# A 64-point transform and two MLPs on one core: the prologue's copies, weight loads and conversions in another order

## The chip, the cores and the metric

The kernel runs on one core of one Trainium2 chip. A core has five engines with an instruction queue each: TensorE (PE in the rows; PEld is its weight load), VectorE (DVE), ScalarE (ACT), GpSimd (POOL) and SyncE (SP), which here only issues DMAs. The 16 DMA engines are shared by all queues. [...] The metric is device time in microseconds (us).

## The reference

What is computed: the real part of a two-dimensional Fourier transform of x (2 batches, 3008 positions, 256 channels), then two MLPs over its 6016 tokens.

```python
X = np.fft.fft(np.fft.fft(x, axis=1), axis=2).real          # (2, 3008, 256) -> tokens (6016, 256)
h = X @ moe_w_in                                            # 256 -> 2048
g = np.maximum(h, 0) + moe_alpha * np.minimum(h, 0)
y = g @ moe_w_out                                           # 2048 -> 256
h2 = y @ moe2_w_in
out = (h2 / (1 + np.exp(-h2))) @ moe2_w_out
```

The host hands the weights over as 64-bit words; the kernel loads them raw and converts them to float32 pairs itself.

## The kernel before

The 3008 positions are split as 47 x 64. A product over the 47 (the position products, tile `psU`) is followed by one over the 64 (tile `psB`), and the transform over channels is folded into the first MLP's input weights (tile `psW`: the product of a converted weight `wq` with the constants `cwt`, split into a high and a low part `wa`). Tokens come in six groups of up to 512 columns; each of the six runs 16 steps of the first MLP (lines 575 to 621), and after all of them the second MLP runs in a second loop (lines 741 to 809). Everything is written in program order (`manual_schedule`); each engine works through its queue in that order, and the framework adds the semaphore waits that the data demand.

The change touches only the prologue, which ends where the loop `for c in range(NC)` begins. In order:

- Ten products of a zero tile (`spin`, line 894) go to PE while the inputs travel.
- SP loads `ac` (the constants of the position products), then the eight parts of x for batch 0, 8 positions each, 384 KB each. Behind part 5 comes the first raw weight, called i0 here (512 KB, the first 256 columns of the first MLP's `w_in`); behind part 7 the raw weights o0 (of `w_out`) and i1 (of `w_in`); then small constants and nine more raw weights. DMAs on SP take eight semaphores in turn, so each issue waits until the DMA eight earlier has landed. ACT issues the loads of `cwt` and `cbt`.
- `stage_u(n)` takes the next n positions (a chunk; `UNITS` lists them: five of 12, one of 4): two PE instructions per position into one of two `psU` buffers (three PSUM banks each), then four copies into `u_all`, alternately by DVE and ACT. Each copy reads one half of psU's partitions (`half`) and writes one half of u_all's (`m`).
- A conversion is a generator (`narrow`, line 203). Its work: two ACT instructions (lines 224 and 225) on the raw words, then three of DVE (230, 232, 234), then `finish`. For `w_out` that is an ACT copy (line 278) and a GpSimd subtraction (line 279). `next` runs it to its next `yield`, `run` to its end. i0 is converted behind chunk 3; psW and its sums psS (line 537) follow behind chunk 4, then the last chunk, then o0's conversion.
- `psB` (line 968): 32 instructions; ACT and DVE split the result into `pq`. A product `psP` (line 979) makes `pb`, ACT copies it, then i1 is converted (`run(first[1])`), and the loop begins: `psh` products (line 575), then on DVE lines 583, 584, 586, 589, and so on. The second psW is the loop's first job.

The tiles `ac`, `con` and `y64` (the float32 result of a conversion) share the two buffers of the tag "y".

```python
for i, (half, m) in enumerate(((0, 0), (1, 0), (0, 1), (1, 1))):
    src = v[half * N2:(half + 1) * N2, :, :, m].rearrange("p b j c -> p c b j")
    dst = uv[m * N2:(m + 1) * N2, :, half, done:done + n].rearrange("p c (b j) -> p c b j", j=4)
    if i % 2: A.activation(dst, src, AF.Copy)
    else: V.tensor_copy(dst, src)
```

Of the kernel before, what the change touches and what calls it, by code (L numbers as in the profile page):

```python
# [30 lines left out]
NX = 8  # L31
# [65 lines left out]
def kernel(  # L97
# [14 lines left out]
    nc = tc.nc  # L112
# [752 lines left out]
    T2 = 14, 16, 19, 22, 50, 51, 52, 53, 54, 56, 58  # L865
    SUB = G
    STEP2 = [0] + [NC * NF + 56 * c for c in range(NC - 1)]
    SPIN = 10,

    BEHIND = 5  # L870
    UNITS = 12, 12, 12, 12, 12, 4
    RAWS = {"o0": (0, "wA2"), "o1": (1, "wA2"), "i2": (0, "px1"), "i3": (1, "px1"), "i4": (0, "wA3"), "i5": (1, "wA3"),
            "o2": (0, "px2"), "o3": (1, "px2"), "i6": (0, "px6"), "i7": (1, "px6")}
    RAW_ORDER = ("i", 2), ("o", 1), ("i", 3), ("o", 2), ("i", 4), ("o", 3), ("i", 5), ("i", 6), ("i", 7)
# [6 lines left out]
    with tc.manual_schedule():  # L881
# [21 lines left out]
        def load_raw(kind, n):  # L903
            i, tag = RAWS[kind + str(n)]
            if tag not in places:
                places[tag] = keep.tile([P, 2, 2, 256, 2], I32, name="raw8", tag=tag)
            raws[kind, n] = t = places[tag][:, i]
            load64(rows_win(n) if kind == "i" else rows_wout(w_out, n), t)

        first = [narrow_win(p) for p in range(2)]  # L910
        for i in range(nx):
            if i % 2 == 0:
                t = keep.tile([2 * NP1, 2, NX, P], F32, name="x0", tag=f"wo1_{i // 2}")
            xr.append(t[:, i % 2])
            nc.sync.dma_start(xr[i], x[0, i])
            if i == BEHIND:
                next(first[0])
        A.dma_start(cwt.rearrange("p k e j -> p (k e j)"), cw)
        A.dma_start(cbts.rearrange("p a e k -> p (a e k)"), cb)
        load_raw("o", 0)  # L920
        next(first[1])
        con = wtile([2 * NP1, 192], F32, "const", "y")
        nc.sync.dma_start(con, ca)
        nc.sync.dma_start(al, alpha)
# [6 lines left out]
        def stage_u(n):  # L931

            nonlocal done
            t = pp.tile([P, 3, 512], F32, name="psU", tag="u", bufs=2)
            for j in range(n):
                i, r = divmod(done + j, NX)
                T.matmul(t[:, j // 4, j % 4 * 96:j % 4 * 96 + 96], xr[i][:, r], ac, start=True, stop=True)  # L937
            v = t[:, :n // 4, :384].rearrange("p b (j m c) -> p b j m c", j=4, m=2)
            for i, (half, m) in enumerate(((0, 0), (1, 0), (0, 1), (1, 1))):
                src = v[half * N2:(half + 1) * N2, :, :, m].rearrange("p b j c -> p c b j")  # L940
                dst = uv[m * N2:(m + 1) * N2, :, half, done:done + n].rearrange("p c (b j) -> p c b j", j=4)
                if i % 2:
                    A.activation(dst, src, AF.Copy)
                else:
                    V.tensor_copy(dst, src)
            done += n

        for i, n in enumerate(UNITS):
            stage_u(n)
            if i == 3:  # L950
                run(first[0])
            if i == 4:
                run(mix_w(0, pp, "o"))
        assert done == N2
        wo0 = narrow_wout(w_out, wo1, "wo1_", 0, 0, raws["o", 0])
        pre.__exit__(None, None, None)
        psh = ctx.enter_context(tc.tile_pool(name="psh", bufs=1, space=PSUM, reuse_waits="tile"))
        pso = ctx.enter_context(tc.tile_pool(name="pso", bufs=4, space=PSUM, reuse_waits="tile"))
        run(wo0)
        ur, cbt = u_all[:, 0], side(0)  # L960
        V.tensor_copy(cat.rearrange("p s m -> p (s m)"), con)
        row = wtile([P, CK, N2], F32, "row0", "h")
# [2 lines left out]
        for eo in range(2):  # L965
# [9 lines left out]
                A.activation(hi, src, AF.Copy)  # L975
            for src, hi, lo in pairs:
                V.tensor_tensor(lo, src, f32(hi), op=ALU.subtract)
        ps = pso.tile([P, CK, N2], F32, name="psP", tag="o")
        T.matmul(ps, ones[:, 0:1].to_broadcast([P, P]), row, start=True, stop=True)
        for dst, src in spread(0, lambda k0, k1, w: ps[:, k0:k1, :w]):  # L980
            A.activation(dst.rearrange("p (k c) -> p k c", c=src.shape[2]), src, AF.Copy)
        A.activation(rest, ps[:, 0, OWN:K20], AF.Copy)
        run(first[1])
        V.tensor_scalar(al, al, -1.0, 1.0, op0=ALU.mult, op1=ALU.add)


# [132 lines left out]
```

## Time and profile before

| what | before |
|---|---|
| median of three timed runs | 993.22 us (992.76 to 995.02) |
| the profiled execution, device time | 992.17 us |
| its span (first to last instruction) | 990.4 us |
| PE busy | 960.8 us, 97% of the span |
| DVE, ACT, POOL busy | 711.6, 592.9, 509.6 us |
| first position product | 5.74 us |
| first psB product | 29.39 us |
| first line 583 on DVE | 41.58 us |

Times in rows are microseconds from the span's start. A row of the timeline gives start, duration, engine, line, operation, output and inputs, shapes and count; in brackets stand the engine's idle time before it and what ended it. [...]

### The profile page before, as it was taken

To read this page: it belongs to the slowest core of one execution; us is meant where nothing else is said; L and a number is where in the kernel's file an instruction comes from. 1 tells how busy PE (TensorE), PEld (TensorE's weight loads), DVE (VectorE), ACT (ScalarE), POOL (GpSimd) and SP (SyncE) were. 2 spreads that over 40 slices of the span, in tenths; PEclk is the share of its full clock that TensorE was granted. 3 is DMA by queue.
4 is the path that set the end of the run, shared out by engine and by line. 5 is a ranking of instruction groups with operands and counts; after the bars stand their busy time and mean duration, and the time that the engine had idled before them with its cause. 6 is when DMAs were issued, how large, how long until landed. Compare 5 with 4: busy or idle time off the path is not lost.

```text
span 990.4 us, 12453 instructions
## 1 busy us (share of the span) xinstructions
PE 960.8 (97%) x4374; PEld 798.8 (81%) x4374; DVE 711.6 (72%) x1099; ACT 592.9 (60%) x1002; POOL 509.6 (51%) x328
## 2 busy tenths in 40 slices
PE   8889899999999999999999999999999999999998
PEld 7778778878878878778789988888888888888886
DVE  3598876779989988998766765576576567657554
ACT  3566556666656656665676565665566465565554
POOL 0144557765545546988996543354354354335222
PEclk9799999999999999999999999999999999999999
DMA  9400113333334210010011020010001001001001
GB/s 284 161 1 22 40 33 81 80 81 93 107 117 118 75 64 23 22 64 22 11 44 32 1 80 1 0 43 1 1 1 43 1 1 43 1 1 44 1 0 43
DMA packets 30430, 46.52 MB, mean 47 GB/s; under 512 B 3264, under 2 KB 13344, under 8 KB 30112
## 3 DMA queue, kind: packets, MB, share of 16 engines
q1 hardware_dynamic: 30080, 45.34, 14.9%
q8 instruction: 34, 0.56, 0.2%
q10 hardware_dynamic: 288, 0.39, 0.1%
q14 instruction: 28, 0.23, 0.1%
HBM read 32.22 MB, written 13.51 MB: 46 GB/s over the span
## 4 chain that ended last, share of the span: by engine, by line
PE 80%; DVE 8%; ACT 4%; POOL 3%; issue 2%; DMA 1%; SPq 0%; ACTq 0%; DVEq 0%; POOLq 0%
PE pso L809 26%; PE psh L741 23%; PE pso L621 18%; PE psh L575 9%; DVE r L589 3%; POOL gl L606 2%; ACT r L585 2%; DVE psh L584 1%; PE psB L413 1%; PE psW L531 1%; ACT gh L605 1%; PE psB L968 1%; PE psU L937 1%; DVE h L583 1%; DVE x L633 1%
## 5 line engine op out<-in xcount | busy, mean ns | idle before, releaser
L762 DVE TENSOR_TENSOR ring<-ring,psh 128x512 f32<-128x512 f32 (+1 forms) x336 | 222.3, 674 | 170.5 <-PE psh L741 161.2
L809 PE MATMUL pso<-ghl,wAo 128*128 128x512 f32 (+1 forms) x1152 | 310.7, 386 | 0.0
L606 POOL TENSOR_TENSOR gl<-r,gh 128x1024 fp32r<-128x1024 f32 (+1 forms) x96 | 227.1, 2366 | 153.6 <-ACT gh L605 117.2
L741 PE MATMUL psh<-ts,wi 128*128 128x512 f32 (+1 forms) x1008 | 280.8, 387 | 0.0
L753 POOL TENSOR_TENSOR ghl<-ring,ghl 128x512 fp32r<-128x512 f32 (+1 forms) x96 | 137.8, 1436 | 254.8 <-ACT ghl L748 181.6
L809 PEld LDWEIGHTS pso<-ghl,wAo 128*128 128x128 f32 x1152 | 216.3, 188 | 42.2
L765 ACT ACTIVATE ring<-ring 128x512 f32<-128x512 f32 (+1 forms) x192 | 119.4, 622 | 178.3 <-DVE ring L762 176.0
L741 PEld LDWEIGHTS psh<-ts,wi 128*128 128x128 f32 x1008 | 189.2, 188 | 36.7 <-DVE r L589 0.2
L621 PE MATMUL pso<-gh,wo_o 128*128 128x512 f32 (+1 forms) x768 | 189.4, 387 | 3.6 <-POOL wo_o L279 3.6
L575 PE MATMUL psh<-pq,wa 128*128 128x512 f32 (+1 forms) x576 | 167.9, 401 | 4.7 <-DVE r L589 4.6
L621 PEld LDWEIGHTS pso<-gh,wo_o 128*128 128x128 f32 x768 | 144.0, 188 | 33.1 <-POOL wo_o L279 4.7
L589 DVE SCALAR_TENSOR_TENSOR r<-r,al,psh 128x512 f32<-128x512 f32 (+1 forms) x192 | 134.0, 734 | 15.9 <-ACT r L585 4.8
L605 ACT ACTIVATE gh<-r 128x1024 fp32r<-128x1024 f32 (+1 forms) x96 | 100.3, 1044 | 68.0 <-DVE r L589 67.7
L575 PEld LDWEIGHTS psh<-pq,wa 128*128 128x128 f32 x576 | 106.1, 190 | 29.1 <-DVE r L589 8.4
L748 ACT ACTIVATE ghl<-ring 128x512 fp32r<-128x512 f32 (+1 forms) x192 | 119.0, 620 | 6.2
L585 ACT ACTIVATE r<-psh 128x512 f32<-128x512 f32 (+1 forms) x96 | 56.4, 588 | 82.8 <-DVE psh L584 77.0
L621 PE MATMUL pso<-gl,wo_o 128*128 128x512 f32 (+1 forms) x384 | 103.5, 391 | 1.9 <-POOL gl L606 1.9
L584 DVE TENSOR_TENSOR psh<-h,psh 128x512 f32<-128x512 f32 (+1 forms) x96 | 65.8, 685 | 47.4 <-PE psh L575 43.1
L621 PEld LDWEIGHTS pso<-gl,wo_o 128*128 128x128 f32 x384 | 72.0, 188 | 18.3 <-POOL gl L606 3.6
L753 DVE TENSOR_TENSOR ghl<-ring,ghl 128x512 fp32r<-128x512 f32 (+1 forms) x96 | 76.9, 802 | 4.0 <-ACT ghl L748 3.6
L583 DVE SCALAR_TENSOR_TENSOR h<-pb,wst,psh 128x512 f32<-128x512 f32 (+1 forms) x96 | 70.0, 730 | 0.0
L586 DVE TENSOR_TENSOR psh<-h,psh 128x512 f32<-128x512 f32 (+1 forms) x96 | 65.1, 679 | 0.0
(91 smaller groups left out, 668.0 us busy)
## 6 DMA issues: line engine op xcount, KB each, us to landing
raw<-in_w_in SPq DMA_DIRECT2D x16, 512.0 KB, 6.3
raw<-in_w_out SPq DMA_DIRECT2D x16, 512.0 KB, 3.8
out_dram<-ob SPq DMA_DIRECT2D x20, 256.0 KB, 2.2
x<-in_x SPq DMA_DIRECT2D x8, 384.0 KB, 9.6
xr<-in_x SPq DMA_DIRECT2D x16, 192.0 KB, 2.5
tmid<-ev SPq DMA_DIRECT2D x48, 64.0 KB, 1.8
ur<-tmid SPq DMA_DIRECT2D x12, 256.0 KB, 3.7
stash_o<-y SPq DMA_DIRECT2D x8, 256.0 KB, 4.0
```

The source lines that it names most:

```text
L575: T.matmul(t[:, :w], wa[q][:, mm, eo, a, :], pq[c][:, 2 * eo + bb, :w], start=n == 0, stop=n == 2)
L583: V.scalar_tensor_tensor(t[:, :w], pb[c][:, :w], wst[:, m, 0:1], ps[0][:, :w], op0=ALU.mult, op1=ALU.add)
L589: V.scalar_tensor_tensor(r[:, s, :w], r[:, s, :w], al[:, m:m + 1], ps[s][:, :w], op0=ALU.mult, op1=ALU.add)
L605: A.activation(hi[:, :, :w], r[:, :, :w], AF.Copy)
L606: G.tensor_tensor(lo[:, :, :w], r[:, :, :w], f32(hi[:, :, :w]), op=ALU.subtract)
L621: T.matmul(po[c][s][k][:, :w], wo1[q][:, mm, a, k * P:(k + 1) * P], g[:, s, :w], start=m == 0 and a == 0 and g is hi, stop=m == NF - 1 and ...
L741: T.matmul(bank[j][:, :w], wi2[p][:, FORMS[j], a], t[:, :w], start=a == 0 and t is hi, stop=t is lo)
L748: A.activation(outs[p, i][:, 0, :w], g[:, :w], AF.Copy)
L753: eng.tensor_tensor(hl[:, 1, :w], g[:, :w], f32(hl[:, 0, :w]), op=ALU.subtract)
L762: V.tensor_tensor(dst[:, :w], a[:, :w], bank[j][:, :w], op=ALU.add)
L765: A.activation(a[:, :w], a[:, :w], AF.Silu)
L809: T.matmul(po[c, 2][s][k][:, :w], wo2[q][:, mm + m, a, k * P:(k + 1) * P], outs[p, i][:, g, :w], start=p == 0 and i < 2 and a == 0 and g == 0,
```

## The change

`SPIN` goes from 10 to 5. Part 0 of x is loaded in two DMAs of 4 positions. The raw weights i0, o0 and i1 are issued behind parts 2, 3 and 4 of x. `UNITS` becomes four chunks of 12, one of 8 and two of 4. The four copies of a chunk are paired in another order, so that DVE writes the lower half of u_all's partitions and ACT the upper half. `AMONG` lists how many steps of which conversion (0: i0, 1: i1, 2: o0) are run behind which chunk, and psW for i0 comes behind chunk 3 instead of chunk 4. The rest of o0's conversion is run between the two halves of psB, and i1's no longer stands ahead of the loop.

```diff
@@ -865,10 +865,11 @@
     T2 = 14, 16, 19, 22, 50, 51, 52, 53, 54, 56, 58
     SUB = G
     STEP2 = [0] + [NC * NF + 56 * c for c in range(NC - 1)]
-    SPIN = 10,
-
-    BEHIND = 5
-    UNITS = 12, 12, 12, 12, 12, 4
+    SPIN = 5,
+
+    BEHIND = {2: ("i", 0), 3: ("o", 0), 4: ("i", 1)}
+    UNITS = 12, 12, 12, 12, 8, 4, 4
+    AMONG = {0: ((0, 3),), 1: ((0, 3),), 2: ((1, 1),), 3: ((1, 5),), 4: ((2, 1),), 6: ((2, 4),)}
     RAWS = {"o0": (0, "wA2"), "o1": (1, "wA2"), "i2": (0, "px1"), "i3": (1, "px1"), "i4": (0, "wA3"), "i5": (1, "wA3"),
             "o2": (0, "px2"), "o3": (1, "px2"), "i6": (0, "px6"), "i7": (1, "px6")}
     RAW_ORDER = ("i", 2), ("o", 1), ("i", 3), ("o", 2), ("i", 4), ("o", 3), ("i", 5), ("i", 6), ("i", 7)
@@ -912,13 +913,16 @@
             if i % 2 == 0:
                 t = keep.tile([2 * NP1, 2, NX, P], F32, name="x0", tag=f"wo1_{i // 2}")
             xr.append(t[:, i % 2])
-            nc.sync.dma_start(xr[i], x[0, i])
-            if i == BEHIND:
-                next(first[0])
+            for a, n in ((0, NX),) if i else ((0, NX // 2), (NX // 2, NX // 2)):
+                nc.sync.dma_start(xr[i][:, a:a + n], x[0, i, :, a:a + n])
+            if i in BEHIND:
+                kind, n = BEHIND[i]
+                if kind == "i":
+                    next(first[n])
+                else:
+                    load_raw(kind, n)
         A.dma_start(cwt.rearrange("p k e j -> p (k e j)"), cw)
         A.dma_start(cbts.rearrange("p a e k -> p (a e k)"), cb)
-        load_raw("o", 0)
-        next(first[1])
         con = wtile([2 * NP1, 192], F32, "const", "y")
         nc.sync.dma_start(con, ca)
         nc.sync.dma_start(al, alpha)
@@ -936,7 +940,7 @@
                 i, r = divmod(done + j, NX)
                 T.matmul(t[:, j // 4, j % 4 * 96:j % 4 * 96 + 96], xr[i][:, r], ac, start=True, stop=True)
             v = t[:, :n // 4, :384].rearrange("p b (j m c) -> p b j m c", j=4, m=2)
-            for i, (half, m) in enumerate(((0, 0), (1, 0), (0, 1), (1, 1))):
+            for i, (half, m) in enumerate(((0, 0), (0, 1), (1, 0), (1, 1))):
                 src = v[half * N2:(half + 1) * N2, :, :, m].rearrange("p b j c -> p c b j")
                 dst = uv[m * N2:(m + 1) * N2, :, half, done:done + n].rearrange("p c (b j) -> p c b j", j=4)
                 if i % 2:
@@ -945,18 +949,18 @@
                     V.tensor_copy(dst, src)
             done += n
 
+        wo0 = narrow_wout(w_out, wo1, "wo1_", 0, 0, raws["o", 0])
         for i, n in enumerate(UNITS):
             stage_u(n)
+            for g, k in AMONG.get(i, ()):
+                for _ in range(k):
+                    next(first[g] if g < 2 else wo0, 0)
             if i == 3:
-                run(first[0])
-            if i == 4:
                 run(mix_w(0, pp, "o"))
         assert done == N2
-        wo0 = narrow_wout(w_out, wo1, "wo1_", 0, 0, raws["o", 0])
         pre.__exit__(None, None, None)
         psh = ctx.enter_context(tc.tile_pool(name="psh", bufs=1, space=PSUM, reuse_waits="tile"))
         pso = ctx.enter_context(tc.tile_pool(name="pso", bufs=4, space=PSUM, reuse_waits="tile"))
-        run(wo0)
         ur, cbt = u_all[:, 0], side(0)
         V.tensor_copy(cat.rearrange("p s m -> p (s m)"), con)
         row = wtile([P, CK, N2], F32, "row0", "h")
@@ -975,12 +979,13 @@
                 A.activation(hi, src, AF.Copy)
             for src, hi, lo in pairs:
                 V.tensor_tensor(lo, src, f32(hi), op=ALU.subtract)
+            if eo == 0:
+                run(wo0)
         ps = pso.tile([P, CK, N2], F32, name="psP", tag="o")
         T.matmul(ps, ones[:, 0:1].to_broadcast([P, P]), row, start=True, stop=True)
         for dst, src in spread(0, lambda k0, k1, w: ps[:, k0:k1, :w]):
             A.activation(dst.rearrange("p (k c) -> p k c", c=src.shape[2]), src, AF.Copy)
         A.activation(rest, ps[:, 0, OWN:K20], AF.Copy)
-        run(first[1])
         V.tensor_scalar(al, al, -1.0, 1.0, op0=ALU.mult, op1=ALU.add)
 
 
```

What this does to the queues. First DVE, from the first position product on: the copies of chunks 0 to 2 before (`psU_148`, `psU_165`, `psU_182`), with the semaphores that each waits for.

```order
L945 COPY u_all_80<-psU_148 64x48x12 [waits PE_49]
L945 COPY u_all_80<-psU_148 64x48x12 [waits Activation_49]
L945 COPY u_all_80<-psU_165 64x48x12 [waits PE_49]
L945 COPY u_all_80<-psU_165 64x48x12 [waits Activation_49]
L945 COPY u_all_80<-psU_182 64x48x12 [waits PE_49]
```

The same place after the change (`psU_144`, `psU_165`, `psU_184` are chunks 0 to 2; `wq_161` is i0's result).

```order
L949 COPY u_all_80<-psU_144 64x48x12 [waits PE_49]
L949 COPY u_all_80<-psU_144 64x48x12 [waits Activation_49]
L230 TENSOR_SCALAR wq_161<-wq_161 128x512 [waits Activation_49]
L949 COPY u_all_80<-psU_165 64x48x12 [waits PE_49]
L949 COPY u_all_80<-psU_165 64x48x12 [waits Activation_49]
L232 ISA wq_161<-raw64_113,wq_161 128x1024 [waits DMAHW7_49,DVE_49]
L234 SCALAR_TENSOR_TENSOR wq_161<-raw64_113,wq_161 128x512 [waits DVE_49]
L949 COPY u_all_80<-psU_184 64x48x12 [waits PE_49]
```

The conversion of i0 now stands between the copies; a chunk's second DVE copy waits for ACT in both.

Next ACT around the last chunks, before: `psU_222` is chunk 4, `psU_251` chunk 5, the last; `y64_267` is o0's result.

```order
L943 ACTIVATE u_all_80<-psU_222 64x48x12 [waits DVE_49] x2
L533 ACTIVATE wa0_239<-psW_240 128x2x2x128 [waits PE_49]
L538 ACTIVATE wst_74<-psS_246 128x4 [waits PE_49]
L943 ACTIVATE u_all_80<-psU_251 64x48x4 [waits DVE_49] x2
L224 ACTIVATE y64_267<-raw8_128 128x512 [waits DMAHW4_49]
L225 ACTIVATE raw8_128<-raw8_128 128x512
L278 ACTIVATE wo1_o0_273<-y64_267 128x2x256 [waits DMAHW2_49,DVE_49]
```

After: `psU_204` is chunk 3, `psU_236` chunk 4, `psU_252` and `psU_261` chunks 5 and 6; `wq_201` is i1's result, `y64_249` o0's.

```order
L224 ACTIVATE wq_201<-raw64_120 128x512 [waits DMAHW3_49]
L225 ACTIVATE raw64_120<-raw64_120 128x512
L947 ACTIVATE u_all_80<-psU_204 64x48x12 [waits DVE_49] x2
L533 ACTIVATE wa0_224<-psW_225 128x2x2x128 [waits PE_49]
L538 ACTIVATE wst_74<-psS_231 128x4 [waits PE_49]
L947 ACTIVATE u_all_80<-psU_236 64x48x8 [waits DVE_49] x2
L224 ACTIVATE y64_249<-raw8_116 128x512 [waits DMAHW1_49,PE_49]
L225 ACTIVATE raw8_116<-raw8_116 128x512
L947 ACTIVATE u_all_80<-psU_252 64x48x4 [waits DVE_49] x2
L947 ACTIVATE u_all_80<-psU_261 64x48x4 [waits DVE_49] x2
```

Line 224 for o0 moved from behind the last chunk's copies to ahead of the copies of the last two, and it now waits for PE too: the last product of chunk 6, which reads the buffer that `y64_249` takes over.

Last SP, from the first part of x on, before (`x0` are the parts, two to a tile; `raw64_121` is i0, `raw8_128` o0, `raw64_130` i1).

```order
L915 DMA x0_112<-in_x 96x1024 x2
L915 DMA x0_115<-in_x 96x1024 x2
L915 DMA x0_118<-in_x 96x1024
L915 DMA x0_118<-in_x 96x1024 [waits DMAHW0_49]
L196 DMA raw64_121<-in_w_in 128x2x512 [waits DMAHW1_49]
L915 DMA x0_123<-in_x 96x1024 [waits DMAHW2_49]
L915 DMA x0_123<-in_x 96x1024 [waits DMAHW3_49]
L196 DMA raw8_128<-in_w_out 128x2x512 [waits DMAHW4_49]
L196 DMA raw64_130<-in_w_in 128x2x512 [waits DMAHW5_49]
```

After (`raw64_113` is i0, `raw8_116` o0, `raw64_120` i1).

```order
L917 DMA x0_107<-in_x 96x512 x2
L917 DMA x0_107<-in_x 96x1024
L917 DMA x0_111<-in_x 96x1024
L196 DMA raw64_113<-in_w_in 128x2x512
L917 DMA x0_111<-in_x 96x1024 [waits DMAHW0_49]
L196 DMA raw8_116<-in_w_out 128x2x512 [waits DMAHW1_49]
L917 DMA x0_118<-in_x 96x1024 [waits DMAHW2_49]
L196 DMA raw64_120<-in_w_in 128x2x512 [waits DMAHW3_49]
L917 DMA x0_118<-in_x 96x1024 [waits DMAHW4_49]
L917 DMA x0_123<-in_x 96x1024 [waits DMAHW5_49]
```

The three weights moved up by three to five places, to stand between the parts of x.

## Rows read from the trace of the kernel before

**Rows 1.** The page: the span, and PE's busy time.
```profile
span 990.4 us, 12453 instructions
...
PE 960.8 (97%) x4374; PEld 798.8 (81%) x4374; DVE 711.6 (72%) x1099; ACT 592.9 (60%) x1002; POOL 509.6 (51%) x328
```

**Rows 2.** Busy time by stretch; behind POOL: granted clock, DMA share, GB/s.
```profile
5.56:20.65 15.09, 14.43 (x122) 13.74 (x120) 6.00 (x8) 5.44 (x9) 0.00 (x0) 1.00 1.04 288
...
29.39:36.45 7.06, 7.06 (x33) 7.06 (x34) 2.77 (x7) 2.52 (x6) 2.29 (x2) 0.50 0.64 236
...
39.70:70.00 30.30, 24.19 (x121) 20.64 (x120) 28.31 (x49) 19.02 (x36) 11.78 (x6) 1.00 0.05 18
```

**Rows 3.** Timeline of PE from the spin to the second psW.
```profile
1.45 4.45 PE L894 MATMUL idle<-zero 128*128 128x512 f32 x10 [1.45 <-DVE zero L885]
...
11.83 5.60 PE L937 MATMUL psU<-const,x 96*128 96x96 f32 x48 [0.30 <-ACT u_all L943]
...
23.11 3.42 PE L531 MATMUL psW<-wq,cwt 128*128 128x256 f32 x8 [2.47 <-DVE wq L234]
26.37 0.50 PE L537 MATMUL psS<-ones,wq 128*128 128x2 f32 x4
...
29.39 7.06 PE L968 MATMUL psB<-cbt,u_all 128*128 128x64 f32 x32 [1.54 <-ACT u_all L943]
...
37.27 2.92 PE L575 MATMUL psh<-pq,wa 128*128 128x450 f32 x6
41.64 1.99 PE L531 MATMUL psW<-wq,cwt 128*128 128x256 f32 x8 [1.45 <-DVE wq L234]
```

**Rows 4.** Timeline: copies of chunk 0, psW's low part, two copies of chunk 5.
```profile
8.88 0.75 DVE L945 COPY u_all<-psU 64x576 f32<-64x576 f32 x1 [7.34 <-PE psU L937]
...
9.67 0.65 ACT L943 ACTIVATE u_all<-psU 64x576 f32<-64x576 f32 x1 [6.72 <-DVE u_all L945]
10.35 0.75 DVE L945 COPY u_all<-psU 64x576 f32<-64x576 f32 x1 [0.71 <-ACT u_all L943]
...
27.20 0.69 DVE L546 TENSOR_TENSOR wa<-psW,wa 128x512 fp32r<-128x512 f32 x1 [2.02 <-ACT wa L533]
...
28.27 0.33 ACT L943 ACTIVATE u_all<-psU 64x192 f32<-64x192 f32 x1 [1.03 <-DVE u_all L945]
28.62 0.35 DVE L945 COPY u_all<-psU 64x192 f32<-64x192 f32 x1 [0.39 <-ACT u_all L943]
```

**Rows 5.** Timeline of SP's issues, each held until the DMA eight earlier landed.
```profile
7.68 0.39 SPq L196 DMA_DIRECT2D raw<-in_w_out  x1
9.12 0.39 SPq L196 DMA_DIRECT2D raw<-in_w_in  x1
...
13.41 0.37 SPq L196 DMA_DIRECT2D raw<-in_w_in  x1
15.20 0.37 SPq L196 DMA_DIRECT2D raw<-in_w_out  x1
...
17.86 0.37 SPq L196 DMA_DIRECT2D raw<-in_w_out  x1
19.10 0.37 SPq L196 DMA_DIRECT2D raw<-in_w_in  x1
```

**Rows 6.** Timeline of ACT and DVE from pb to the loop's first instructions.
```profile
38.29 0.63 ACT L981 ACTIVATE pb<-psP 128x33 f32<-128x33 f32 x2 [1.11 <-PE psP L979]
...
38.89 0.68 ACT L224 ACTIVATE wq<-raw 128x512 f32<-128x512 f32 x1
39.44 0.69 ACT L225 ACTIVATE raw<-raw 128x512 int32<-128x512 uint32 x1
39.60 0.43 DVE L230 TENSOR_SCALAR wq<-wq 128x512 int32<-128x512 int32 x1 [1.59 <-ACT wq L224]
...
41.58 0.68 DVE L583 SCALAR_TENSOR_TENSOR h<-pb,wst,psh 128x450 f32<-128x450 f32 x1
...
42.36 0.63 DVE L584 TENSOR_TENSOR psh<-h,psh 128x450 f32<-128x450 f32 x1
```

## The prediction, as it was put on record

> **What bounds the kernel now.** I read the page first: TensorE (PE) is busy for 97% of the span, so over the whole kernel PE is the limit [rows 1]. The change touches only the prologue, so the next view is the table of stretches. [...] Then the engines one by one: PE's timeline for what it does and waits for [rows 3], the copies of a chunk [rows 4], the SP queue, whose issue times tell when inputs landed [rows 5], and the conversion ahead of line 583 [rows 6].
>
> **Copies in halves.** Today a chunk's four copies stand in one chain: DVE at 8.88, ScalarE (ACT) at 9.67, DVE again at 10.35, each after the other engine's, 1.47 us a pair, 2.94 us for twelve positions [rows 4]. Two engines side by side would need 2 x 0.75 = 1.5 us. But the built order of the changed kernel still has the same waits: DVE's second copy waits for Activation, both ACT copies wait for DVE. The chain stays, and this edit is worth 0.
> [...] In the old order the first DVE copy and the first ACT copy read different halves of psU's partitions and still do not overlap [rows 4]. [...]
>
> **Half the spin, and part 0 of x in two DMAs.** Ten spin products take 4.45 us [rows 3], so five end near 3.7 us and the first position products can start when the first half-part lands, about 4. Nothing comes of it: the first chunk needs part 1, which landed at 7.68 (the SP issue at 7.68 waits for it; with eight semaphores each issue waits for the DMA eight earlier) [rows 5]. Four positions are 8 products of 0.117 us (48 in 5.60) [rows 3], so chunk 0 ends near 8.9 as now. The cover of these edits is part 1's transfer. What the shorter spin costs if the clock has not risen is the first rival.
>
> **Three weights between x's parts.** Parts 3 to 5 of x now stand behind one weight each, part 3 behind i0, part 4 also behind o0, part 5 also behind i1. Parts landed 1.43 us apart ((13.41 - 9.12) / 3); a weight cost 1.79 between parts (15.20 - 13.41) and 1.24 behind the last (19.10 - 17.86) [rows 5]. I take 1.6, nearer to the first, since these too lie between parts. Part 2 stays at 9.12; then part 3 lands at 12.15, part 4 at 15.2, part 5 at 18.2, and parts 6 and 7 are no limit. Chunk 3 ends 8 positions (16 x 0.117 = 1.9 us) after part 5: 20.1. Today PE is done with five chunks by 20.65.
>
> **psW between chunks, conversions in the gaps.** From 20.1: the psW products follow at once, since i0 is converted long before; 2.0 us at the higher clock (the row at 41.64; 3.42 at the lower, the row at 23.11), 0.5 for psS [rows 3], 1.9 for the 8 positions of chunk 4: 24.4. DVE is later than that: chunk 3's copies run 20.1 to 23.0, DVE's last at 22.3, then i1's three instructions (some 1.9, as from 39.60 to line 583) [rows 6] to 24.2 and the low part of psW (0.69) [rows 4] to 24.8. Chunk 4's four copies, sized between the 0.75 of twelve positions and the 0.35 of four [rows 4], take 2.2: 27.0. Now the new tail. Chunk 6 needs chunk 4's psU buffer, so its 8 products run 27.0 to 28.0. In ACT's order o0's two conversions stand ahead of the copies of chunks 5 and 6, and the first has a new wait on PE: the buffer "y" held the constants that all position products read, so it waits for chunk 6's last product. It runs 28.0 to 29.25 (1.24, rows 38.89 and 39.44) [rows 6]. Queued behind it: ACT's half of chunks 5 and 6, for which DVE's halves wait, and psB waits for all. Six links are left, four of ACT (0.33) and two of DVE (0.35) with 0.04 between [rows 4]: 2.15. psB starts at 31.4 in place of 29.39 [rows 3]: **2.0 us later**. The bounds go with the weights' price: at 1.24 each, part 5 lands 1.1 earlier and psB starts near 30.6; at 1.79, near 32.0.
>
> **What psB no longer waits for.** PE has 3.4 us without work ahead of psB, so I keep psB at the lower clock, 7.06 us: today it is at 0.50 [rows 2] after 1.54 without work (the bracket at 29.39) [rows 3]. After psB, DVE today does i1's conversion, and only then line 583 at 41.58 and 584 at 42.36 [rows 6]. That conversion is gone from here. Line 583 needs pb, written by 38.92 [rows 6], and line 584 the sixth psh product, done at 37.27 + 2.92 = 40.2 [rows 3]. So line 584 comes at 40.2 instead of 42.36: **2.15 us earlier** against psB's start. o0's DVE part still runs under psB, and its GpSimd part, now behind "row", has all of psB, psP and the first steps before the second layer reads it; without that cover it would cost its 1.3 us. The second psW starts after the psh products instead of at 41.64, some 0.6 later, but its reader on DVE stands behind the next conversion and hides that. The remaining raw loads keep their number and end before the loop wants them, as SP's last ones do today.
>
> **Sum.** +2.0 - 2.15 = -0.15 us, from -1.0 to +0.5 by the weights' price. The profiled execution took 992.17 (span 990.4 and 1.8 around it), so 992.0 on its scale. The three timed runs have a median of 993.22, 1.05 above it; on that scale 993.1, with 991.6 to 995.0 as this case's own range (a stretch at the other clock moves 1.4 us: psW's 3.42 against 1.99). A step of 0.2%, 2.0 us, is about what a measurement can tell from no change: the three runs differ by 2.3.
>
> **Rivals.**
> *Slower: the clock does not rise (0.14).* [...] Five spins and then half-size work with a wait may not raise it; psB, unbroken for 7 us, did not [rows 2]. No row has position products at the lower level; psW's ratio 3.42 / 1.99 = 1.72 makes 0.117 into 0.20, the bounds being 0.117 and 0.234. 128 products then take 25.6 us from 4.0, psW 3.4 and psS 0.5: 33.5 instead of 28.0 for chunk 6, and with the same tail 5.5 to 6.5 us more: about 999.2. It decides if the clock is still low when part 3 lands at 12; until then PE waits for x anyway.
> [...]
> *Slower: the clock falls in the new gaps between parts (0.11).* PE waits about 1.2 us before parts 4 and 5. A fall doubles some 2 us of position products and may make psW 3.42: +2.5 to 3.5, 995.6 to 996.4. For it: 2.47 us without work came ahead of the slow psW and 1.54 ahead of the slow psB [rows 3]. Against: each new gap is shorter than either.
> *Faster: the clock is high in psB (0.09).* 7.06 / 1.72 = 4.1, so -3.0: 990.1. Against it stands the longer gap ahead.
> *Faster: the halves do run side by side (0.03).* Chunk 4's chain and the last six links halve, -2.2: 990.9. The waits in the order speak against it. That this edit does nothing is my forecast.
>
> **How the numbers follow.** Forecast 0.63. Within 0.2%: 0.63; faster, the last two rivals, 0.12; slower, the first two, 0.25. The likeliest time is 993.1. The range 990.0 to 996.5 takes in all but the first rival and some of the tails.
>
> **What would show it.** Right: ACT's u_all copies still start after DVE's; position products of chunk 3 wait for x; line 224 for o0 starts after chunk 6's last product; psB starts at 30.6 to 32.0 at clock 0.50; line 584 within 1 us of 42.4, and after it the same distances as before. Wrong: psU products at 0.2 us, copies of one chunk overlapping, psB in about 4 us, or parts of x that land at their old times in spite of the weights.

## The result: 0.85% slower

The changed kernel takes 1001.34 us (median of 4 runs, 1000.58 to 1001.96), the kernel before 992.99 (median of 4, 990.5 to 995.02): ratio 1.0085, 95% interval 1.0061 to 1.0109, 8.4 us more. The forecast was 993.1 with a range to 996.5. The time lies 2.1 us above that of the prediction's first rival, "the clock does not rise" (999.2, chance 0.14).

PE's timeline after (start, duration, count; in brackets idle time and what ended it) answers [rows 3]:

```profile
1.45 2.50 PE L895 MATMUL idle<-zero 128*128 128x512 f32 x5 [1.45 <-DVE zero L886]
4.78 20.77 PE L941 MATMUL psU<-const,x 96*128 96x96 f32 x96 [0.82 <-DMA x<-in_x]
25.34 3.67 PE L531 MATMUL psW<-wq,cwt 128*128 128x256 f32 x8
28.80 0.73 PE L537 MATMUL psS<-ones,wq 128*128 128x2 f32 x4
29.40 2.90 PE L941 MATMUL psU<-const,x 96*128 96x96 f32 x24
33.67 1.13 PE L941 MATMUL psU<-const,x 96*128 96x96 f32 x8 [1.37 <-ACT u_all L947]
38.32 7.09 PE L972 MATMUL psB<-cbt,u_all 128*128 128x64 f32 x32 [3.52 <-ACT u_all L947]
46.23 3.24 PE L575 MATMUL psh<-pq,wa 128*128 128x450 f32 x6
```

96 position products in 20.77 us are 0.216 each; before, 48 took 5.60, 0.117 each. The second set here, 24 products behind psW in 2.90, is at 0.121 again. The traces show two levels of the granted clock, 1.00 and 0.50 [rows 2]; so it was at the lower one through chunks 0 to 3 and psW (3.67 us, against 1.99 at 1.00 [rows 2, 3]), and rose only behind psW, at 29.27. PE waited for nothing in between: chunk 3 ends at 25.5 where 20.1 was forecast, and psB starts 8.93 us later than before (38.32 against 29.39).

The loop's first DVE instructions in the changed kernel answer [rows 6]:

```profile
48.46 0.68 DVE L583 SCALAR_TENSOR_TENSOR h<-pb,wst,psh 128x450 f32<-128x450 f32 x1 [1.43 <-PE psh L575]
49.51 0.63 DVE L584 TENSOR_TENSOR psh<-h,psh 128x450 f32<-128x450 f32 x1 [0.36 <-PE psh L575]
```

Line 584 comes 7.15 us later than 42.36: 8.93 from psB's start, less 1.78 that the way from psB to line 584 became shorter (12.97 to 11.19). Of the 9.3 us between the spans (999.7 and 990.4) the rest, 2.1, is lost in the loop (its steps are the 96 passes through line 584, counted from 0): 1.5 between steps 15 and 17, where the clock fell once more behind a pause of 1.77 us, and 0.6 in steps 40 to 48. The first of these two places, after and before:

```profile
137.43 2.12 PE L621 MATMUL pso<-gh,wo_o 128*128 128x450 f32 x7 [1.77 <-POOL wo_o L279]
139.34 1.49 PE L575 MATMUL psh<-pq,wa 128*128 128x512 f32 x3
```

```profile
130.27 1.69 PE L621 MATMUL pso<-gh,wo_o 128*128 128x450 f32 x7 [1.78 <-POOL wo_o L279]
131.80 0.86 PE L575 MATMUL psh<-pq,wa 128*128 128x512 f32 x3
```

The same pause stands in both, but the products behind it are slow in one only. Of the 18 profiles of this case 13 have this fall and 5 do not, with long and short prologues among both, so it is not counted as an effect of the change. The 0.6 is no sure effect either: from step 39 to 50, 16 of the other 17 profiles lose 0.05 to 3.3 us against this one execution of the kernel before, early prologues and late ones.

SP's issues after answer [rows 5]; an issue still waits for the DMA eight earlier, and these wait for part 3, o0, part 4, i1 and part 5:

```profile
11.93 0.35 SPq L928 DMA_DIRECT2D al<-in_alpha  x1
13.45 0.39 SPq L196 DMA_DIRECT2D raw<-in_w_in  x1
14.93 0.37 SPq L196 DMA_DIRECT2D raw<-in_w_out  x1
16.45 0.37 SPq L196 DMA_DIRECT2D raw<-in_w_in  x1
17.96 0.37 SPq L196 DMA_DIRECT2D raw<-in_w_out  x1
```

Part 5 landed at 17.96, 7.6 us before PE was done with it: at the lower clock PE, not x, is late.

### The profile page after: what moved, and what is told of

Same layout as the page of the kernel before. It is cut to its first block, busy times and chain, and to the rows that moved or that the text cites. A ratio compares the mean times of both kernels' runs of the same rounds, so it can differ in the third digit from the quotient of the medians.

```text
span 999.7 us, 12454 instructions
## 1 busy us (share of the span) xinstructions
PE 970.9 (97%) x4369; PEld 808.8 (81%) x4369; DVE 711.9 (71%) x1101; ACT 593.3 (59%) x1004; POOL 510.0 (51%) x328
## 4 chain that ended last, share of the span: by engine, by line
PE 79%; DVE 10%; ACT 4%; POOL 2%; DMA 2%; issue 2%; SPq 0%; ACTq 0%; DVEq 0%; POOLq 0%
PE pso L809 26%; PE psh L741 23%; PE pso L621 16%; PE psh L575 9%; DVE r L589 4%; PE psU L941 2%; ACT r L585 2%; POOL gl L606 2%; DVE psh L584 1%; DVE h L583 1%; DMA stash_o<-y 1%; PE psB L413 1%; DVE y L234 1%; PE psW L531 1%; ACT gh L605 1%
```

## Experiments

Each time is a median with its range, each ratio is to the kernel before on the same chip, with its 95% interval.

### The two suspects, one at a time

**Ten spins in the changed kernel.**

```diff
-    SPIN = 5,
+    SPIN = 10,
```

> The changed kernel with ten spin products again in place of five; all else of the change stays. Clock theory: the position products fall from 0.216 to about 0.117 us each, part 5 of x sets the end of chunk 3 (about 20), psB starts at 30.6 to 32.0, line 584 at about 42.4, and the time is 992 to 994, 7 to 9 us below the changed kernel. Rival (weights between the parts, the new tail or the new copy order cost the time): position products may get faster, but line 584 stays behind 46 and the time is above 998.

Measured: 999.5 us (997.48 to 1001.24), ratio 1.0064 (1.0052 to 1.0077). Only 1.8 us came back, and the clock theory in this simple form fell. Busy time by stretch (behind POOL: granted clock, DMA share, GB/s):

```profile
5.75:9.00 3.25, 2.38 (x19) 2.05 (x18) 0.00 (x0) 0.00 (x0) 0.00 (x0) 1.00 1.03 254
9.00:25.78 16.78, 16.78 (x80) 16.78 (x80) 6.24 (x9) 6.31 (x10) 1.06 (x1) 0.50 1.05 285
```

The clock rose, as it does before, and fell at 9.0: in the 3.25 us ahead of that, PE had worked 2.38 and waited twice for parts of x.

```profile
5.75 1.03 PE L941 MATMUL psU<-const,x 96*128 96x96 f32 x8
7.00 1.13 PE L941 MATMUL psU<-const,x 96*128 96x96 f32 x8 [0.22 <-DMA x<-in_x]
8.78 17.21 PE L941 MATMUL psU<-const,x 96*128 96x96 f32 x80 [0.65 <-DMA x<-in_x]
```

From there the products are again at 0.215. So these runs show two ways to the lower clock: it does not rise (in the changed kernel not before 29.27), or it falls behind pauses of PE (here at 9.0, behind 0.22 and 0.65 us). The prediction's second rival has the second way, but in the gaps ahead of parts 4 and 5. In this execution the clock fell earlier: eight products are four positions, so the two waits are for the second half of part 0 and for part 1, which SP issues ahead of all weights. The gaps ahead of the later parts show in other runs below.

**Five spins in the kernel before.**

```diff
-    SPIN = 10,
+    SPIN = 5,
```

> The kernel before with five spin products in place of ten and nothing else. Clock theory: position products at about 0.216 us; the first five chunks (120 products) end near 30.7 instead of 20.65, line 584 comes 6 to 9 us later than 42.36, and the time is 999 to 1002. Rival (the five products are harmless by themselves and only together with the weights between the parts or the half-sized first transfer does the clock stay low): products at 0.117 us, time 993 within 1.

Measured: 1002.92 us (1001.24 to 1003.47), ratio 1.0096 (1.0083 to 1.0109).

```profile
5.87 25.89 PE L937 MATMUL psU<-const,x 96*128 96x96 f32 x120 [1.92 <-DMA x<-in_x]
40.16 7.09 PE L968 MATMUL psB<-cbt,u_all 128*128 128x64 f32 x32 [1.54 <-ACT u_all L943]
```

120 position products at 0.216, and line 584 at 53.17, 10.8 us late. The halved spin alone costs more than the whole change, 9.6 us against the median of the kernel before on that chip (993.35).

**The three weights between the parts, in the kernel before.**

```diff
-    BEHIND = 5
+    BEHIND = {2: ("i", 0), 3: ("o", 0), 4: ("i", 1)}
```

> The kernel before with one part of the change: the three weights i0, o0 and i1 between x's parts (behind parts 2, 3 and 4); ten spins, the old conversions, the old tail. Theory (the prediction's landing times, with the fall of the clock in the gaps that ten spins showed): part 5 lands near 18.2 in place of 13.4, chunk 3 ends near 20.5 in place of 17.4, psB starts 2.5 to 5 us after 29.39 and the time is 996 to 999, scattered by several us from execution to execution. Rival (the weights between the parts are covered by the copies and by i0's conversion, which psW waits for): psB within 1 us of 29.39, time 993 to 994.

Measured: 999.84 us (996.02 to 1004.32), ratio 1.0065 (1.0041 to 1.0088).

```profile
11.92 2.00 PE L939 MATMUL psU<-const,x 96*128 96x96 f32 x16 [0.69 <-DMA x<-in_x]
14.90 2.97 PE L939 MATMUL psU<-const,x 96*128 96x96 f32 x16 [0.99 <-DMA x<-in_x]
18.10 8.85 PE L939 MATMUL psU<-const,x 96*128 96x96 f32 x40 [0.23 <-DMA x<-in_x]
```

After waits of 0.69 and 0.99 us the last 40 products take 0.221 each; the granted clock is 0.50 from 15.77 on, and psB starts at 35.35. With ten spins and the old tail the weights alone cost 6.5 us, by the later parts and the lower clock together. The two losses do not add (9.6, 6.5, and 8.4 for the whole change). The rows show one reason: at the lower clock from the start PE waits for no part any more (96 products in 20.77 us, and 120 in 25.89, without a pause). How much the change's other edits give back was not separated.

### The tail and the copies

**o0's first step behind the last chunk** (ten spins).

```diff
-    AMONG = {..., 4: ((2, 1),), 6: ((2, 4),)}
+    AMONG = {..., 6: ((2, 5),)}
```

> The changed kernel with ten spin products, and o0's first step (line 224, which waits for chunk 6's last product) moved from behind chunk 4 to behind the last chunk. By the prediction's term for the new tail, psB starts about 2.0 us earlier than with ten spins alone (near 29.4 against 31.4), line 584 near 40.4, and the time is 2.0 lower, about 991. Rival (ACT's conversion then falls into psB's stretch and holds up ACT's first work behind psB, or the chunk copies set psB's start anyway): psB less than 0.7 us earlier, same time.

Measured: 996.8 us (993.37 to 1002.67), ratio 1.0038 (1.002 to 1.0056): 2.7 below ten spins alone. The wait ahead of psB is 1.55 us in place of 3.51:

```profile
32.06 7.09 PE L972 MATMUL psB<-cbt,u_all 128*128 128x64 f32 x32 [1.55 <-ACT u_all L947]
```

The profiled execution, the fastest of nine, kept the clock high until 17.3, between waits of 0.70 and 0.87 us for parts 4 and 5, which is why its psB (32.06) can't be compared directly. In the rows the term for the tail, 2.0, held. The medians agree with it, but their two intervals overlap, so 2.7 is no better figure.

**The old pairs of copies** (ten spins).

```diff
-            for i, (half, m) in enumerate(((0, 0), (0, 1), (1, 0), (1, 1))):
+            for i, (half, m) in enumerate(((0, 0), (1, 0), (0, 1), (1, 1))):
```

> The changed kernel with ten spin products and the old pairing of the four copies of a chunk (DVE on the first half of psU's partitions, ACT on the second). Theory of the prediction: the copies stand in one chain either way, so psB starts within 0.3 us of the run with ten spins alone, and the time is the same within 0.1%. Rival (the new pairing by itself saves or costs something): copies of a chunk overlap in one of the two, and psB moves by 1 us or more.

Measured: 1000.19 us (998.4 to 1001.66), ratio 1.0077 (1.0064 to 1.009), the same as ten spins alone. Its psB starts 3.3 us earlier (35.37), but because the clock fell later, at 15.7, in the gap ahead of part 4 (1.23 us, after one of 1.09 ahead of part 3): by psB's start alone this run could not be judged, since the moment of the fall differs between executions of like kernels. In the changed kernel itself the chain is plain:

```profile
10.22 0.75 DVE L949 COPY u_all<-psU 64x576 f32<-64x576 f32 x1 [8.67 <-PE psU L941]
11.01 0.64 ACT L947 ACTIVATE u_all<-psU 64x576 f32<-64x576 f32 x1 [8.05 <-DVE u_all L949]
11.68 0.76 DVE L949 COPY u_all<-psU 64x576 f32<-64x576 f32 x1 [0.71 <-ACT u_all L947]
```

### What raises the clock, and what keeps it

**Five spins, and ten more products of the spin's form ahead of part 3.**

```diff
                 i, r = divmod(done + j, NX)
+                if r == 0:
+                    spin({3: 10}.get(i, 0))
```

> The changed kernel as it is (five spins), with ten more products of the spin's form ahead of part 3 of x, that is behind 48 position products. [...] Rival (too little time has passed, or the clock does not rise in this part whatever PE does): position products at 0.216 to the end, ten products more in their way, time 1003 to 1005.

Measured: 1000.28 us (1000.2 to 1000.86), ratio 1.0073 (1.0058 to 1.0087).

```profile
5.15 10.53 PE L943 MATMUL psU<-const,x 96*128 96x96 f32 x48 [1.19 <-DMA x<-in_x]
15.38 3.52 PE L895 MATMUL idle<-zero 128*128 128x512 f32 x10
18.74 5.49 PE L943 MATMUL psU<-const,x 96*128 96x96 f32 x48
```

48 position products without a pause, 0.219 each; ten products of 512 columns, during which the clock rose (between 15.38 and 18.74); then 48 position products at 0.114. The rival is out: the place in the prologue and the time that has passed are the same in the changed kernel, where the products still took 0.216 there. The time hardly followed: the ten products took 3.5 us themselves, chunk 6 waited 2.77 us for copies, and psB came at 37.39, 0.9 earlier than in the changed kernel.

**Ten spins, PE kept busy while it waits for x.**

```diff
+                if r == 0:
+                    spin({3: 3, 4: 5, 5: 5}.get(i, 0))
```

> The changed kernel with ten spin products, and PE kept busy while it waits for x behind a weight: three products of the spin's form ahead of part 3, five ahead of parts 4 and 5 (0.21 us each at the higher clock). Gap theory (with ten spins alone the clock rose and fell again in the gaps that the weights between the parts make): the granted clock stays 1.00 to psW, chunk 6 ends near 28, psB starts at 30.6 to 32.0, and the time is 992 to 994.5 in nearly every execution, where ten spins alone gave 997.5 to 1001.2. Rival (the clock falls for another reason, such as the position products' own 96 columns): position products at 0.2 us after some 3 to 10 us again, time as with ten spins alone or above.

Measured: 997.27 us (993.61 to 998.65), ratio 1.0038 (1.0026 to 1.005). The products do keep the clock: psW takes 1.92, and the last position products 0.121. But psB starts at 34.77 and the time is above the range that was expected. In this execution parts 4 and 5 landed at 17.5 and 21.2, 2.6 and 3.2 us later than in the changed kernel with the same order of DMAs, and chunk 3 ended at 23.2. It is not alone in that: part 5 landed at 20.33 with ten spins alone and at 21.15 in the run before this one. Why the parts are late in some executions is not explained. PE waits for them, so psB starts later by it. From chunk 6's end to psB it is 3.5 us, as forecast (3.4).

**The same with o0's step late and products ahead of chunk 6 and psB.**

```diff
+            for _ in range({56: 6, 60: 7}.get(done, 0)):
+                T.matmul(t[:, 2], zero[:, :P], zero, start=True, stop=True)
```

> As the last one (ten spins, products of the spin's form ahead of parts 3, 4 and 5), with o0's first step behind the last chunk, and such products also in the two waits of the new tail: six ahead of chunk 6, seven ahead of psB. Clock theory: psB starts near 29.5, at 1.00 takes 4.1 us, line 584 comes at 37 to 38.5 and the time is 987.5 to 990, below the kernel before. Rival (psB runs at the lower clock whatever stands ahead of it): psB 7.1 us, time 990.5 to 992. Second rival (the additional products delay the position products): psB later than 31.

Measured: 1000.63 us (997.13 to 1002.95), ratio 1.0072 (1.0048 to 1.0096); psB 3.69 us long, but at 39.92, as in the second rival. The experiment was badly built: the additional products write psU's tile, and so wait for ACT's copies out of it:

```profile
30.64 2.93 PE L954 MATMUL psU<-zero 128*128 128x512 f32 x6 [3.14 <-ACT u_all L949]
36.77 3.32 PE L954 MATMUL psU<-zero 128*128 128x512 f32 x7 [1.55 <-ACT u_all L949]
```

### One weight only between the parts

**i0 alone between the parts** (ten spins, o0's step late; i1 and o0 behind part 7).

```diff
-    BEHIND = {2: ("i", 0), 3: ("o", 0), 4: ("i", 1)}
+    BEHIND = {2: ("i", 0)}
-    AMONG = {..., 2: ((1, 1),), 3: ((1, 5),), ...}
+    AMONG = {..., 4: ((1, 1),), 5: ((1, 5),), 6: ((2, 5),)}
```

> The changed kernel with ten spins, o0's first step behind the last chunk, and only i0 between x's parts; i1 and o0 stand behind part 7, and i1's conversion in the gaps of chunks 4 and 5. Theory (what is left of the loss, some 3 us, comes from the parts of x behind weights, by their landing and by the clock that falls meanwhile): the granted clock stays at 1.00 until the new tail, chunk 3 ends by 18.5, psB starts at 27.5 to 29.5, line 584 at 38 to 40.5, and the time is 989 to 991.5, below the kernel before. Rival (the order of the conversions or the seven chunks cost it): psB after 31, time 995 or above.

Measured: 997.98 us (992.77 to 1000.41), ratio 1.0048 (1.003 to 1.0065). The profiled execution, 992.77, has the clock of the theory, high until 27.16, but chunk 3 ends at 19.4 (18.5 expected) and psB starts at 31.09 (29.5 at the latest): PE waits 4.13 us for ACT's copies ahead of it. The seven others lie at 997.6 to 1000.4. Their mean granted clock is 0.982 to 0.986 against 0.991: 0.007 less is an estimated 14 us more at the lower level (0.007 / 0.5 x 991). With all three weights between the parts and the same late step of o0 the median was 996.8, so taking two of them out gained nothing in the common executions. A second profile was to be one of those:

> The kernel with one weight between x's parts once more, for its profile: the execution profiled before took 992.77 with the clock high until 27.16, while the seven timed ones took 997.6 to 1000.4. Clock theory: this profile is of the common kind, near 998, and its granted clock falls between 9 and 20, so that position products, psW and psS run at the lower level; everything else is as in the first profile. Rival: the clock is as in the first and another wait makes the 5 us.

Measured: 991.97 us, with the clock high until 25.0, so no profile shows the common executions from inside. What makes them slow was therefore tested by changing it:

```diff
                 i, r = divmod(done + j, NX)
+                spin({24: 3, 36: 3}.get(done + j, 0))
...
+            if i == 6:
+                spin(6)
             stage_u(n)
...
         assert done == N2
+        spin(16)
```

> The kernel with one weight between x's parts, with products of the spin's form in PE's four pauses: three ahead of part 3 of x, three in chunk 3, six ahead of chunk 6, sixteen ahead of psB (pauses of 0.77, 0.72, 1.56 and 4.13 us in its profile). Clock theory: PE's pauses in the prologue decide the clock; with these products it stays high, psB takes 3.8 us, line 584 comes at 38 to 39 and the time is 988.5 to 991, scattered by no more than 4 us. Rival (something other than PE's pauses makes the common executions slow): median 994 or above.

Measured: 990.85 us (989.37 to 991.7), ratio 0.9972 (0.9961 to 0.9983).

```profile
24.07 1.64 PE L895 MATMUL idle<-zero 128*128 128x512 f32 x6
25.85 1.13 PE L944 MATMUL psU<-const,x 96*128 96x96 f32 x8
26.76 3.90 PE L895 MATMUL idle<-zero 128*128 128x512 f32 x16
31.13 3.79 PE L979 MATMUL psB<-cbt,u_all 128*128 128x64 f32 x32 [0.47 <-ACT u_all L950]
```

Products that compute nothing take 7.1 us off and shrink the scatter from 7.6 to 2.3 us. They write a tile of their own (allocated anew behind psW), so no copy is waited for. None of the six executions is near 998 any more, so PE's pauses made the common ones slow. Which of the four pauses does it was not separated, and part of the gain is psB's, 3.79 us in place of 7.09: it ran at the lower clock in the two profiles without the early fall too.

**i0's conversion behind chunk 3 again.**

```diff
-    AMONG = {0: ((0, 3),), 1: ((0, 3),), ...}
+    AMONG = {3: ((0, 6),), ...}
```

> The kernel with one weight between x's parts, with i0's conversion behind chunk 3 (as in the kernel before) in place of in the gaps of chunks 0 and 1. Theory A (a conversion between two chunks' copies holds the copies, so PE waits for psU's buffers and the clock falls): with the conversion behind chunk 3 position products keep the higher clock to the end of chunk 3 in most executions, psW waits for i0's conversion as before, and the median is 994 to 995.5, below 997.98. Theory B (only the weight in the middle of x matters): median within 1 of 998.

Measured: 1004.3 us (1002.28 to 1007.27), ratio 1.0107 (1.0091 to 1.0124). Neither theory:

```profile
12.99 9.09 PE L943 MATMUL psU<-const,x 96*128 96x96 f32 x48 [1.16 <-DMA x<-in_x]
27.77 3.78 PE L531 MATMUL psW<-wq,cwt 128*128 128x256 f32 x8 [5.69 <-DVE wq L234]
```

The clock fell at 14.6 all the same, so it falls without the conversions in the gaps too; and psW waited 5.69 us for i0. The early conversion of i0 is a good part of the change, worth 6.3 us with one weight between the parts (1004.3 against 997.98).

### The kernel before with the pauses filled

**Products ahead of psW and of psB**, the second in psU's tile.

```diff
             if i == 4:
+                spin(11)
                 run(mix_w(0, pp, "o"))
...
+            for _ in range(7 if done == 60 else 0):
+                T.matmul(t[:, 2], zero[:, :P], zero, start=True, stop=True)
```

> The kernel before, with products of the spin's form (512 columns, into a tile that nobody reads) where PE stands idle in the prologue: eleven ahead of psW (idle for 2.47 us) and seven ahead of psB (1.54). They do no work of the result. Clock theory (after short pauses PE's lower clock is what costs): granted clock 1.00 over psW, which takes 2.0 in place of 3.42, and over psB, 4.1 in place of 7.06; line 584 some 3 to 4 us before 42.36 and the time 989 to 990. Rival (psB is at the lower clock because of its own products, not of the pause ahead): psB stays at 7.06, at most 1 us gained.

Measured: 990.33 us (988.84 to 995.27), ratio 0.9976 (0.9962 to 0.9989). psW takes 1.99, psB 3.68 in place of 7.06 [rows 3]: psB is slow for what precedes it, not by itself.

```profile
30.91 3.68 PE L971 MATMUL psB<-cbt,u_all 128*128 128x64 f32 x32
```

**The seven in a tile of their own.**

```diff
         assert done == N2
+        idle = pp.tile([P, 512], F32, name="idle", tag="o")
+        spin(7)
```

> The kernel before with products of the spin's form in PE's two pauses as in the earlier run (eleven ahead of psW, seven ahead of psB), but the seven write a tile of their own: in the earlier run they wrote psU's tile, waited for ACT's copies (2.21 us) and put psB off from 29.39 to 30.91. Clock theory: they start when the last chunk's products end, psB starts within 0.5 us of 29.4, takes 3.7 us, line 584 comes at 38.4 to 39.2, and the time is 988.5 to 989.5, some 1 us below the earlier run. Rival (DVE's conversion of i1, not PE, decides line 584 by now): line 584 near 40, time as in the earlier run, 990.3.

Measured: 991.75 us (989.74 to 993.51), ratio 0.9983 (0.9974 to 0.9993). psB starts at 29.12 as meant, but line 584 at 40.36, as in the rival. A wait that psB used to hide is in the open now:

```profile
34.86 1.39 PE L982 MATMUL psP<-row,ones 128*128 128x512 f32 x2 [1.97 <-POOL row L966]
35.42 3.08 PE L575 MATMUL psh<-pq,wa 128*128 128x450 f32 x6
```

**i1's conversion early.**

```diff
-        run(wo0)
+        next(wo0)
+        next(first[1])
+        run(wo0)
+        run(first[1])
```

> The last kernel with one part of the change taken over: i1's conversion (two instructions on ACT, three on DVE) stands behind o0's, ahead of DVE's work on psB, in place of ahead of line 583. Prediction's term for that conversion (2.15 us): DVE idles under psB, so the conversion is hidden there and line 584 comes 1.5 to 2.2 us earlier than in the last kernel, time 986.5 to 988. Rival (it pushes DVE's and ACT's work on psB back by as much): line 584 less than 0.5 us earlier, same time.

Measured: 990.91 us (989.31 to 992.37), ratio 0.9978 (0.9968 to 0.9989); line 584 at 39.70, 0.66 earlier. The conversion is off the path (line 583 now waits 1.79 us for psh), and GpSimd's row takes its place: psP waits 2.67 us, and the psh products behind it are slow (3.24). The time is not lower: 986.5 to 988 was expected.

**Ten products ahead of psP.**

```diff
+        idle = pso.tile([P, 512], F32, name="idle", tag="o")
+        spin(10)
         ps = pso.tile([P, CK, N2], F32, name="psP", tag="o")
```

> The kernel before with products of the spin's form in PE's pauses and i1's conversion early, and ten more such products ahead of psP, where PE waits 2.67 us for GpSimd's row. Clock theory: psP takes 1.1 in place of 2.07, the first psh products 1.8 in place of 3.24, line 584 comes near 38.2 in place of 39.70, and the time is about 989.5, 1.5 below that kernel. Rival (DVE's and ACT's work on psB decides line 584): line 584 moves by less than 0.5 us.

Measured: 991.32 us (987.99 to 993.35), ratio 0.998 (0.9968 to 0.9991). psP 1.12, psh 1.79, line 584 at 38.09, 1.6 earlier: all as expected, and yet no gain. In the profile (992.73, one of the slower executions) line 584 leads the kernel before by 4.27 us at step 0, by 2.65 at step 17 (the fall of the clock at that place), by 1.35 at step 40, and lags by 0.6 at step 50. ACT's waits between 225 and 300 us, before and here (total, times, longest):

```profile
ACT y L224 <- DMA stash_i<-y: 1.4, 1, 1.4
ACT y L224 <- DMA stash_o<-y: 0.7, 1, 0.7
```

```profile
ACT y L224 <- DMA stash_o<-y: 3.0, 3, 1.3
ACT y L224 <- DMA stash_i<-y: 2.0, 1, 2.0
```

ACT's conversions there wait for writes of the last weight to memory: 5.0 us in place of 2.1. The kernel with one weight and filled pauses shows it too, smaller (3.6; from a lead of 5.0 at step 0, 3.5 at step 39, 1.8 at the end). So a good part of what these two prologues gain is gone at the end of the loop. That an early prologue causes the late writes is not shown: the kernel with o0's step late and products ahead of chunk 6 and psB, 5.3 us behind at step 39, loses 2.2 more by step 50 and has 4.2 us of these waits in the same steps, while the kernel before with the seven in a tile of their own, 1.7 ahead at step 39, loses 0.05. What delays the writes stays open. The five versions that beat both kernels lie at 990.3 to 991.8, close enough that their order is not settled.

## Why the prediction was wrong

On the profile's scale the forecast was 992.0 and the measured time 1001.5. Of some 9.5 us between them 6.9 stand ahead of psB, 0.4 between psB and line 584, and 2.1 in the loop. The forecast lets the end move with line 584: DVE, which works off that line, is busy for 28.31 of 30.30 us in the loop's first steps and PE for 24.19 [rows 2]. Measured, 7.15 of the 9.3 us between the spans stand at line 584.

- **Half the spin: the step that failed.** "Nothing comes of it" took part 1's landing as the cover and left the clock to a rival. Five spins in the kernel before, with nothing else changed, price it: 9.6 us. In the changed kernel it shows as 0.216 us a position product where the forecast had 0.117. The trace of the kernel before had the signs: its ten spins [rows 3] took 0.445 to 0.792 us each, with a median of 0.628, where products of the same 128x512 in its second loop (line 809), at 1.00, have a median of 0.389, so most of the spin ran at the lower level; and psB's unbroken products ran at 0.50 [rows 2]. They are the nearest to position products behind a short spin and spoke for the rival, so 0.14 was too low. Its working was good: 0.20 a product (measured 0.216), chunk 6 done at 33.5 (34.8), psB 5.5 to 6.5 late against the forecast's 31.4 (6.9). The prediction's own sign of being wrong, "psU products at 0.2 us", is what came. The first rival's reading, that five spins may be too little, agrees with the measurement, and 20.8 us of position products without a pause did not raise the clock either.
- **Three weights between the parts.** In the changed kernel's profile the landings were as forecast: 11.93, 14.93 and 17.96 against 12.15, 15.2 and 18.2, 1.5 us a weight. That was in part luck: in the seven other profiles with all three weights between the parts part 5 landed at 18.1 to 21.2, in five of them beyond the forecast's upper price of a weight. The consequence was wrong: the rival "clock falls in the new gaps" (0.11) is what three kernels with ten spins show (old pairs, late step of o0, weights alone); with ten spins alone the clock fell ahead of these gaps. "Each new gap is shorter than either" did not protect them: with the weights alone the clock fell behind waits of 0.69 and 0.99 us. The rival's size was small too. It let a fall double some 2 us of position products; with the weights alone the last 40 took 8.85 us, and the cost was 6.5 in place of 2.5 to 3.5.
- **The new tail.** As forecast: line 224 for o0 starts at 34.84, after chunk 6's last product; from there to psB 3.5 us (forecast 3.4). Taking o0's step out of it shortens the way from chunk 6's end to psB by 2.0 us (3.5 to 1.5).
- **i1 no longer ahead of line 583.** Forecast -2.15, measured -1.78; line 584 waits for psh products, which took 3.24 in place of 2.92.
- **Copies in halves.** Worth 0, as forecast, and still one chain (copies at 10.22, 11.01 and 11.68 in the changed kernel). Both pairings are alike to the measurement (999.5 with the new one and 1000.19 with the old, both with ten spins).
- **psB at the lower clock**: right, 7.09 us.
- **After the prologue** nothing was forecast to move. 2.1 us did, 1.5 of it by a fall of the clock that other kernels of this case have or have not.
- **Two sums** of the prediction do not close: by its own steps a weight at 1.24 gives psB at 30.3, not 30.6, and 3.5 on top of the forecast is 996.6, not 996.4. Neither changes what went wrong.

## What to carry to other kernels

Products that only keep PE busy can be part of the work (here five fewer of them cost 9.6 us): before shortening them, or opening a pause in the work behind them, price the whole stretch at the lower clock and ask which row shows that it will not come to that. Where a clock decides, one profile is one execution (here one of 991.97, where timed ones of the same kernel took 997.6 to 1000.4): judge a kernel by its timed runs and their scatter, and test by filling the pauses. And follow a gain from the prologue through the loop to the end, since later waits can take part of it back (here ACT waited 5.0 us for writes in place of 2.1).

## What was not expected

- 96 position products ran without a pause for 20.8 us, PE busy all the time, and the clock stayed at the lower level; with ten products of 512 columns put behind 48 of them it rose (0.219 to 0.114 a product).
- The clock falls at different moments in kernels that hardly differ: at 9.0 with ten spins, at 15.7 with the copies' pairs changed as well, at 17.3 with the tail changed as well. With equal code the two profiles of the kernel with one weight have it at 27.2 and 25.0, while that kernel's other executions take 5 us longer; and the kernel with the tail changed varies by 9 us (993.37 to 1002.67), where the kernel before varies by some 4.5 on one chip.
- The table of stretches shows 1.00 for the changed kernel's chunks 0 to 3, although the products' 0.216 us says otherwise: its first recorded change of clock is at 29.27, and ahead of that the column can't be relied on here. The mean clock of a span inherits this: it is 0.989 for the changed kernel and 0.997 for the slower kernel before with five spins. The products' duration is the safer reading.

```profile
4.78:25.34 20.56, 20.56 (x97) 20.56 (x97) 6.25 (x9) 6.31 (x10) 1.06 (x1) 1.00 1.04 308
```
